# Twenty matmuls of a blank tile before the first key transposes

## The chip, the cores and the metric

The kernel runs on one core of one Trainium2 chip. A core has a matmul engine (PE, with its weight loads shown apart as PEld), a vector engine (DVE), an activation engine (ACT), a general engine (POOL), a sync engine (SP) and 16 DMA engines. The metric is the device time of one execution, in microseconds; lower is better. The time given for a kernel is the median of its runs.

## The reference

The program is an attention with two kinds of heads, followed by a two-layer network with SiLU. Batch is 8, heads 8, sequence 576, head dimension 64.

```python
scores = scale * np.matmul(q, k.transpose(0, 1, 3, 2))
rel = pos[:, None] - pos[None, :]
mask_plain = (rel >= 0) & (rel < window)                 # window = 32: heads 0-3
mask_dil = (rel >= 0) & (rel < window * dilation) & (rel % dilation == 0)   # dilation = 4: heads 4-7
scores = np.where(masks[None, :, :, :], scores, -1000000000.0)
attn = softmax(scores)                                   # max, exp, sum, divide
attn_out = np.matmul(attn, v)
...
h = x @ w_in                                             # x: 4608 x 512, w_in: 512 x 2048
g = h * (1.0 / (1.0 + np.exp(-h)))
return (g @ w_out).astype(np.float32)                    # w_out: 2048 x 512
```

`x` is the attention's output with the heads of a token side by side.

## The kernel before, in words

Only a band of the scores is not masked, so the kernel works on blocks of 32 queries by 64 keys. The code calls the plain heads z = 0 and the dilated heads z = 1; for the latter, positions are sorted into four classes by remainder, so that their masked scores become a band as well. For each batch b the kernel loads q, k and v, turns q and k so that the head dimension lies on partitions, computes block scores, takes maximum, exponential and sum, turns the probabilities, multiplies them with v, and runs the two layers on the 576 tokens.

The order of the instructions is written out by hand (`manual_schedule`): each engine executes in the order in which the code names its instructions, and waits for the tiles that it needs. From batch 1 on, the attention of the next batch is laid between the matmuls of the current batch's layers by a table of steps (`plan_of`). Batch 0 has nothing to hide behind, and its attention is written out in a straight sequence ahead of the first layer.

What happens up to the first layer, with the lines of the code before the change:

- POOL issues all loads. The first four are k and q of batch 0's dilated heads, then k and q of its plain heads (`load_one`, L112), then v (L154, L163), the four pieces of w_in (L171), q and k of batch 1 (L119, L112), the four pieces of w_out (L177) and v of batch 1. All are cast from float32 to float16 on the way.
- DVE clears a small tile `band` (L184) and the margins of the key and query tiles (L208 to L211); POOL makes the identity and the band mask.
- PE waits for the first k and transposes it (`transpose`, L258), then the first q; ACT and DVE copy the results out of PSUM (L309). `scores0` writes the mask into PSUM by a matmul with the identity (L396) and adds the scores to it (L354 for dilated heads, L338 for plain ones). DVE takes the negated maximum (L413), ACT the exponential (L519, or L508 when DVE has subtracted the maximum in `shift0`, L428), DVE the sum (L527), reciprocal and product (L538 to L541) and the turn of the probabilities (L557). PE multiplies with v (L588), and ACT or DVE copy that into `xT` (L657, L662). Batch 0 is cut into two parts of 256 and 320 tokens, and each part has both kinds of heads.
- The first layer of batch 0 (`layer1_part`, L696) goes over 256 tokens in four groups of 16 matmuls with 256 columns, one group for each piece of w_in, then over the other 320 tokens. Between its groups stand the rest of batch 0's attention and the attention of batch 1. ACT computes SiLU (L704). The second layer is `layer2_first` (L716), and L725 and L726 store the results. For later batches the layers are at L671 and L740, and scores at L327 and L338.
- `warm` (L631) issues n matmuls of the identity with itself into a PSUM tile whose content is overwritten later. The code calls it three times: 3 before the values of the first dilated part, 2 before those of the first plain part, and 3 before the first layer.

PSUM has eight banks. The pool `ps` holds four buffers of one bank, and the pool `big` two buffers of two banks, which the scores of batch 0 and the results of the layers use in turn:

```python
big = ctx.enter_context(tc.tile_pool(name="big", bufs=2, space=bass.MemoryType.PSUM))
...
band = cpool.tile([P, KB], F32, name="band")
nc.vector.memset(band[0:W], 0.0)
tiles_qk(0)
load_one(0, 1, 1)
load_one(0, 1, 0)
make_identity(nc, ident)
```

In these lines P is 128, KB is 64, W is 32, and SA, used by the change, is 256.

Of the kernel before, what the change touches and what calls it, by code (L numbers as in the profile page):

```python
# [8 lines left out]
F16 = mybir.dt.float16  # L9
F32 = mybir.dt.float32  # L10
# [6 lines left out]
P = 128  # L17
# [12 lines left out]
def kernel(  # L30
# [9 lines left out]
    nc = tc.nc  # L40
# [13 lines left out]
    SA = NS // 2  # L54
# [6 lines left out]
    cpool = ctx.enter_context(tc.tile_pool(name="const", bufs=1))  # L61
# [7 lines left out]
    big = ctx.enter_context(tc.tile_pool(name="big", bufs=2, space=bass.MemoryType.PSUM))  # L69
# [110 lines left out]
        )  # L180


    band = cpool.tile([P, KB], F32, name="band")
    nc.vector.memset(band[0:W], 0.0)  # L184
    tiles_qk(0)
# [736 lines left out]
```

## Time and profile before

| what | value |
|---|---|
| median of the runs shown | 306.98 us (306.69 to 309.01, 3 runs) |
| the profiled execution's own time | 306.95 us |
| its span, first to last instruction | 305.1 us |
| PE busy | 292.7 us, 96% of the span |
| DVE, ACT, POOL busy | 199.7, 206.4, 119.6 us |
| PE's first matmul | 5.61 us, after the first k |
| first matmul of layer 1 | 19.69 us |

The page divides the span into 40 equal slices of 7.6 us; a digit is the busy share of an engine in one slice, in tenths. The row PEclk gives the clock that was granted to PE in the same way. The page's chain is followed back from the last instruction, at each step to what released it. A line such as "L696 PE MATMUL h<-xT,w_in 128*128 128x256 f16 x14" means 14 matmuls of code line 696 that write the tile h from xT and w_in, with a weight of 128x128 and 256 moving columns. A bracket behind a line of the timeline is the idle time of the engine before it and what ended it. Matmuls overlap, so a group's length is the distance of its first and last start, and the length of one more.

### The profile page before, as it was taken

Reading aid. Unit: us, or ns where it says so; the run is one execution under the profiler, and the core shown is the slowest. Engines: PE = TensorE matmul, PEld = TensorE weight load, DVE = VectorE, ACT = ScalarE, POOL = GpSimd, SP = SyncE. Lnnn points to the kernel's source line nnn. Section 1 sums busy time; section 2 is a strip of 40 time slices with the busy share of each in tenths; the row PEclk is TensorE's granted clock in tenths of the full one; section 3 lists DMA queues with packets and bytes.
Section 4 is the critical chain, followed back from the end, with each engine's and each line's share of the span. In section 5 each row is a group of like instructions: output and inputs, shape, how many; then the busy total and the mean of one; then the engine's idle time right before and its main releaser. Section 6 shows DMA issues by size and latency. Waiting matters only on the chain.

```text
span 305.1 us, 10290 instructions
## 1 busy us (share of the span) xinstructions
PE 292.7 (96%) x4400; PEld 186.9 (61%) x4400; DVE 199.7 (65%) x354; ACT 206.4 (68%) x688; POOL 119.6 (39%) x182
## 2 busy tenths in 40 slices
PE   2889999999999999999999999999999999999995
PEld 2458654577545774477645775477644775477544
DVE  2886589538898868966895768966895762820012
ACT  2497687865999559965894559975795559546200
POOL 8745347979964295336806086250000000000000
PEclk9999999999999999999999999999999999999999
DMA  6999999999994899499949199390002001110021
GB/s 109 158 205 206 208 157 170 189 185 126 118 184 87 89 70 128 119 106 41 126 71 184 37 62 134 106 118 4 3 34 105 37 2 36 54 52 0 19 86 69
DMA packets 111805, 30.47 MB, mean 100 GB/s; under 512 B 95520, under 2 KB 107280, under 8 KB 111760
## 3 DMA queue, kind: packets, MB, share of 16 engines
q0 software_dynamic: 106432, 20.38, 80.7%
q1 hardware_dynamic: 5328, 9.44, 8.5%
q8 instruction: 34, 0.56, 0.7%
q14 instruction: 11, 0.09, 0.1%
HBM read 40.75 MB, written 9.44 MB: 164 GB/s over the span
## 4 chain that ended last, share of the span: by engine, by line
PE 69%; DMA 16%; POOL 5%; DVE 4%; ACT 3%; issue 2%; POOLq 0%
PE h L671 32%; PE o L740 31%; DMA w_out<-in_moe_w_out_dram 5%; DMA n<-in_q_dram 5%; DMA w_in<-in_moe_w_in_dram 4%; PE x L588 3%; ACT pe L519 2%; DMA n<-in_k_dram 2%; PE s L327 2%; POOL n L132 2%; POOL n L112 1%; DMA vw<-in_v_dram 1%; DVE pn L541 1%; POOL w_in L171 1%; DVE ob L725 1%
## 5 line engine op out<-in xcount | busy, mean ns | idle before, releaser
L679 ACT ACTIVATE gT<-h 128x576 f16<-128x576 f32 x112 | 73.0, 651 | 60.5 <-PE h L671 60.4
L740 PE MATMUL o<-w_out,gT 128*128 128x512 f16 (+1 forms) x528 | 113.8, 373 | 0.0
L671 PE MATMUL h<-xT,w_in 128*128 128x288 f16 x896 | 113.4, 286 | 0.0
L671 PEld LDWEIGHTS <-w_in 128*128 128x128 f16 x896 | 86.6, 98 | 23.5 <-issue 0.2
L740 PEld LDWEIGHTS <-gT 128*128 128x128 f16 x528 | 50.7, 98 | 55.4
L519 ACT ACTIVATE pe<-ms,nm 128x64 f32<-128x64 f32 x238 | 78.9, 333 | 0.1
L725 DVE COPY ob<-o 128x512 f32<-128x512 f32 (+1 forms) x35 | 22.8, 664 | 45.4 <-PE o L740 44.1
L519 ACT ACTIVATION_READ_ACCUMULATOR pe<-ms,nm 128x1 f32 x238 | 44.5, 187 | 0.0
L132 POOL DMA_DIRECT2D n<-in_k_dram x44 | 31.9, 736 | 26.2 <-DVE kC L300 25.1
L372 DVE SCALAR_TENSOR_TENSOR ms<-s,mask 128x512 f32<-128x512 f32 x28 | 19.2, 686 | 28.6 <-PE s L327 19.9
L132 POOL DMA_DIRECT2D n<-in_q_dram x44 | 31.9, 735 | 3.5 <-DMA n<-in_q_dram 3.1
L154 POOL DMA_DIRECT2D vw<-in_v_dram x32 | 18.4, 580 | 34.4 <-PE x L588 31.8
L541 DVE TENSOR_TENSOR pn<-pe,r 128x640 f16<-128x640 f32 (+2 forms) x32 | 25.3, 792 | 1.1
L557 DVE STREAM_TRANSPOSE pt<-pn 128x640 f16<-128x640 f16 (+4 forms) x32 | 24.7, 772 | 1.1
L163 POOL DMA_DIRECT2D vw<-in_v_dram x32 | 21.1, 665 | 9.7 <-DMA w_out<-in_moe_w_out_dram 8.0
L439 DVE TENSOR_REDUCE nm<-ms 128x10 f32<-128x640 f32 (+1 forms) x28 | 22.0, 786 | 1.0
L696 PE MATMUL h<-xT,w_in 128*128 128x256 f16 (+1 forms) x128 | 18.6, 302 | 0.0
L588 PEld LDWEIGHTS <-vw 32*64 32x64 f16 (+1 forms) x1264 | 13.1, 107 | 7.4 <-issue 6.7
L588 PE MATMUL x<-pt,vw 32*64 32x64 f16 (+2 forms) x1264 | 15.0, 193 | 0.9 <-DVE pt L557 0.8
L696 PEld LDWEIGHTS <-w_in 128*128 128x128 f16 x128 | 12.7, 103 | 3.9 <-issue 0.2
L623 DVE CAST xT<-x 128x288 f16<-128x288 f32 x22 | 15.0, 819 | 0.0
L716 PE MATMUL o<-w_out,gT 128*128 128x512 f16 x64 | 14.7, 380 | 0.2 <-ACT ob L725 0.2
(84 smaller groups left out, 209.7 us busy)
## 6 DMA issues: line engine op xcount, KB each, us to landing
out_dram<-ob SPq DMA_DIRECT2D x35, 256.0 KB, 3.0
n<-in_k_dram POOLq DMA_DIRECT2D x24, 108.0 KB, 4.8
n<-in_q_dram POOLq DMA_DIRECT2D x24, 108.0 KB, 5.3
vw<-in_v_dram POOLq DMA_DIRECT2D x31, 80.0 KB, 3.7
vw<-in_v_dram POOLq DMA_DIRECT2D x32, 72.0 KB, 4.0
w_in<-in_moe_w_in_dram POOLq DMA_DIRECT2D x4, 512.0 KB, 9.3
w_out<-in_moe_w_out_dram POOLq DMA_DIRECT2D x4, 512.0 KB, 11.7
n<-in_k_dram POOLq DMA_DIRECT2D x20, 72.0 KB, 3.7
```

The costliest lines, as they stand in the source:

```text
L132: nc.gpsimd.dma_start(out=qk[b, z, which][o : o + QB], in_=bass.AP((q, k)[which].tensor, (b * H + z * HH + half * HH // 2) * S * D + x * Q ...
L163: nc.gpsimd.dma_start(out=vw[h * QB : h * QB + QB, 0:NB], in_=v[b, h].rearrange("(m p) d -> p m d", p=QB))
L439: nc.vector.tensor_reduce(out=nm[:, 0:w], in_=ms[:, 0:w], axis=AX.X, op=ALU.max, negate=True)
L519: nc.scalar.activation(pe[:, t, :], src[t], AF.Exp, bias=a["nm", z, hi][:, t : t + 1], scale=k, accum_out=l[:, t : t + 1],)
L541: nc.vector.tensor_tensor(pn[:, 0:w], a["pe", z, hi][:, 0:w], r[:, 0:w, None].broadcast_to([P, w, KB]), ALU.mult)
L557: nc.vector.transpose(out, src)
L588: nc.tensor.matmul(x[h // 2][h % 2 * D : h % 2 * D + D, col : col + wd], vws[b % 2][r, NB + kb * DIL + c if z else kb], turned_cols(b, pt[ ...
L671: nc.tensor.matmul(h[:, half, 0:HS], w_in16[:, c, f * P : f * P + P], xT[:, c, half * HS : half * HS + HS], start=(c == cs[0]), stop=(c == ...
L679: nc.scalar.activation(gT[:, f, s0 : s0 + S].rearrange("p (a c) -> p a c", a=2), h[:, :, 0:HS], AF.Silu)
L696: nc.tensor.matmul(hs[i // m][:, i % m, 0 : c1 - c0], w_in16[:, c, (f + i) * P : (f + i + 1) * P], xT[:, c, c0:c1], start=(c == 0), stop=( ...
L725: copy(ob, o)
L740: nc.tensor.matmul(o[:, 0, 0:m], gT[:, f, t * P : (t + 1) * P], w_out16[:, f, cols], start=(f == 0), stop=(f == NFF - 1),)
```

## The change

Before anything else of the written-out part, the kernel allocates a float16 tile `blank` of 128 x 256, has DVE fill it with zeros, takes a buffer of the pool `big`, and has PE multiply the blank tile twenty times: a 128x128 piece of it as the weight, all 256 columns as the moving operand, into the first bank of the buffer. Nothing reads this result. The lines below it, and every other function, stay as they were and move down by five lines.

```diff
+    blank = cpool.tile([P, SA], F16, name="blank")
+    nc.vector.memset(blank, 0.0)
+    first_big = big.tile([P, 2, 512], F32, tag="big", name="blank_out")
+    for _ in range(20):
+        nc.tensor.matmul(first_big[:, 0, 0:SA], blank[:, 0:P], blank, start=True, stop=True)
     band = cpool.tile([P, KB], F32, name="band")
     nc.vector.memset(band[0:W], 0.0)
     tiles_qk(0)
```

In the order of instructions, DVE gets one more at its head, PE gets twenty weight loads and twenty matmuls at its head, and POOL, ACT and SP have the same instructions in the same order.

## The prediction

> **What bounds the kernel now.** I read the page first: the span, the slices and the chain.
>
> ```profile
> span 305.1 us, 10290 instructions
> ...
> PE   2889999999999999999999999999999999999995
> ...
> PEclk9999999999999999999999999999999999999999
> ...
> PE 69%; DMA 16%; POOL 5%; DVE 4%; ACT 3%; issue 2%; POOLq 0%
> ```
>
> PE, the matmul engine, is full from the fourth slice on; only the first three slices (0 to 23 us) and the end have holes, so whatever the change brings must be brought before 23 us. Next come PE's own waits:
>
> ```profile
> PE t L258 <- DMA n<-in_k_dram: 5.6, 1, 5.6
> PE x L588 <- DVE pt L557: 0.8, 2, 0.5
> PE t L274 <- DMA n<-in_q_dram: 0.7, 1, 0.7
> PE s L396 <- ACT pe L519: 0.4, 1, 0.4
> PE s L327 <- DVE qC L300: 0.4, 1, 0.4
> ```
>
> The first is the 5.6 us in which the change puts its work. It cannot be shortened, because it ends with k's landing; every other wait is under 1 us. Then the timeline of the first 30 us, where columns are start, length, engine, line, operation, count and the wait before:
>
> ```profile
> 0.90 0.17 DVE L208 MEMSET kC<- 128x128 uint32 x1
> ...
> 5.61 1.14 PE L258 MATMUL t<-ident,n 96*128 96x96 f16 x12 [5.61 <-DMA n<-in_k_dram]
> ...
> 12.24 0.68 DVE L527 TENSOR_REDUCE l<-pe 128x8 f32<-128x512 f32 x1
> 12.38 0.50 PEld L338 LDWEIGHTS <-qT 64*32 64x32 f16 x32 [0.79 <-DVE qT L278]
> 12.38 0.68 PE L338 MATMUL s<-kT,qT 64*32 64x64 f16 x32 [0.31 <-DVE qT L278]
> ...
> 13.12 0.69 DVE L413 TENSOR_REDUCE nm<-s 128x8 f32<-128x512 f32 x1 [0.20 <-PE s L338]
> ...
> 18.00 0.61 PE L631 MATMUL x<-ident 128*128 128x256 f16 x2
> 18.53 0.61 PE L588 MATMUL x<-pt,vw 32*64 32x64 f16 x32
> 19.07 0.82 PE L631 MATMUL h<-ident 128*128 128x256 f16 x3
> 19.69 3.23 PE L696 MATMUL h<-xT,w_in 128*128 128x256 f16 x14
> ...
> 25.43 1.92 PE L696 MATMUL h<-xT,w_in 128*128 128x256 f16 x16
> ...
> 27.29 0.53 PE L588 MATMUL x<-pt,vw 32*64 32x32 f16 x44
> ```
>
> The two L696 lines are the same matmul at two speeds. Single rows follow each other every 213 ns up to 22.73 us and every 109 ns behind it, and one lasts 417 ns before and 272 ns after. So PE runs at half speed from its first instruction to 22.77 us. The PEclk row reads 9 throughout and hides this: the trace's clock record holds nothing earlier than 22.77 us, reads full from there to 306.07 us, and half behind that. A faster clock before 22.77 is all that blank matmuls can bring.
>
> **The change part by part.**
> *The memset.* It fills 512 bytes per partition, as the quoted L208 memset does in 0.17 us. The DVE memsets behind it end near 1.76 instead of 1.59 us; their readers start at 4.71 (POOL, band) and 6.31 us (the kC copy). Cost nothing; the cover would have to shrink by 3 us.
>
> *Twenty matmuls.* The nearest rows are L631: a 128x128 weight, 256 columns, every 213 ns at the slow clock, with loads of 102 to 151 ns beside them. PE waits for the memset, which takes DVE's first place (0.81 us), so they start near 1.1 us and stream for 20 x 0.213 = 4.27 us, to 5.4 us. PE is released by k at 5.61, so 0.2 us is left. An overrun would be taken up by the waits for q: 0.24 us before the second transposes, 0.74 us before 10.84. I take zero; the bounds are 0 and 0.3 us.
>
> *The buffer.* blank_out takes the first of the two "big" PSUM buffers, so each later user takes the other one. The order of reuse is the same, and as PE alone touched the blank, no other engine must release it. Nothing. No DMA is issued, moved or waited for anew; POOL and SP keep their order.
>
> *The clock.* Two questions: does it rise, and does it stay? Neither is in the trace, so bounds. For the rise: PE ran without a hole from 12.38 to 15.1 us (2.7 us) and stayed slow, and without a hole from 16.64 to the rise at 22.7 (6.1 us). The blanks give 4.3 us, between the two. But much of both stretches uses 32 or 64 rows; of full-size work the successful one had the 3.7 us from 19.07, and 4.3 is more. I take it that it rises. For the stay: behind the last matmul, which ends at 301.8 us, the half-clock record comes at 306.07, so 4.3 us of idleness was enough to drop it. From 5.6 to 19 us the longest hole would be near 1.3 us (0.74 now, and faster work before it). I take it that it stays.
>
> The Trainium skill ("TensorE: Matmul & The Clock Gate", section "What's actually happening") says that the clock is released after one busy window of about 3.4 us, and that these windows run freely, not from the kernel's start. The trace agrees: 306.07 - 22.77 = 283.30 us is 83 windows of 3.413 us. By that rule a burst of 4.27 us holds a whole window for only a quarter of the phases, so for the others the sum would be zero unless a partly filled window is enough. The same page ("Part 4: PE-mode transpose") holds that transposes don't count as activity, and the two windows behind the blanks are mostly transposes; by it the clock could drop again, which is the second rival.
>
> *The sum with a fast clock from 5.6 us on.* Landings don't move: from its first load until 88 us POOL waits for nothing but DMAs.
> (a) Up to layer 1 the work passes through DVE and ACT. DVE gives up only its waits on PE: 0.13 us before the qT copy (11.44 to 11.57, shorter transposes) and 0.20 us before the reduce at 13.12. There L338's 32 matmuls, 0.68 us now, would take 0.41 us, as 32 of that line at 41.20 us do, but DVE's L527 then ends last. Together 0.33 us. From 13.12 to 19.19 us ACT's exponentials and DVE set the pace.
> (b) Layer 1's first 32 matmuls: the second is released at 20.00 us, and the 32nd starts at 24.61, 30 spacings in 4.61 us. At 109 ns they take 3.27, a gain of 1.34; with (a) 1.67 us.
> (c) What is late next: the last piece of w_in.
>
> ```profile
> 13.96 12.27 DMA w_in<-in_moe_w_in_dram
> ```
>
> In the chain this transfer ends at 26.23 us; the group that needs it starts at 27.74 now and would be ready at 26.07. Just before, the values at 27.29 need the DVE transpose that ends at 26.03, or 25.70 with (a); PE would be there at 25.62. These leave a start near 26.28, so **1.46 us** is gained. The second piece (20.98 us) and the third (23.35) are in time.
> (d) Behind it nothing takes it back. The next landings are early by the trace's records: batch 1's q at 29.04 against its use near 29.5, w_out's last piece at 42.41 against 51, v at 45.98 against 50.2. The chain's "DMA" up to 70.5 us is no bound: the tile of L300 had landed by 55.7, and DVE was busy with L439 until 70.6, itself behind PE's scores at 67.06. That moves along with PE.
>
> The profiled execution took 306.95 us around its span of 305.1, and the runs shown have a median of 306.98 (306.69 to 309.01), the same. 306.95 - 1.46 = **305.5 us**, 0.5% less. A measurement of this kernel tells a change from none at about 1%, so even full success lies within it.
>
> **The rivals.**
> *The clock never rises* (the change doesn't do what it says). For: 2.7 us was too little, and 4.3 is not 6.1. Against: full-size matmuls. Nothing else moves: 306.95 us.
> *It rises, drops before 19 us, and rises again as now.* For: in 5.7 to 19 us the work, once fast, fills perhaps a third of PE's time. Against: no hole is near 4.3 us. At most (a) is kept: 306.6 us.
> *It drops, and the next rise comes later than 22.77 us: slower.* The place is L696. If the second group of 16 is slow too, 17 matmuls pay 104 ns more, 1.77 us, less the 0.33 of (a): 308.4 us. It turns slower once the fast spacing begins more than about 3 matmuls (0.33 / 0.104) later than now. The one run of 309.01 says that the start of this program can vary by as much; the low 306.69 and 306.95 say that it rarely does.
>
> **How the numbers follow.** Rise 0.7 times stay 0.75: the forecast 0.53. Never rises 0.22. Rises and drops 0.12. Late rise 0.08. Left over 0.05, half of it for an overrun that costs. The forecast's own range is 304.9 (no wait in c, and a little from later stages) to 306.0 us (two thirds of it). To hold 8 in 10 the range must take in the two cases without gain and their run-to-run spread: 304.8 to 307.4 us. Over 1% faster would be under 303.9, more than full speed can give: 0.03. Over 1% slower is above 310.0, worse than the late rise: 0.04. Within 1%: 0.93.
>
> **What would show it.** In the changed kernel's profile 20 matmuls end before 5.6 us; the first L258 rows last near 206 ns instead of 281 if the clock has risen; L696 has 109 ns spacing from its first row, and no row of 417; PE waits for w_in at about 26 us; DVE's reduce at 13.12 comes at 12.8. If L696 starts slow, the clock did not rise or stay, and L258's rows tell which. I am wrong if the gain appears and is lost before 60 us, or if a landing moves.

## The result: slower, and the profile after

The changed kernel takes 309.56 us (308.32 to 313.23, 15 runs) beside 306.94 us for the kernel before on the same chip (306.15 to 310.13, 15 runs). The ratio, taken without the one run of 313.23 us, which stands apart from the others, is 1.0078, with a 95% interval of 1.0053 to 1.0103. The prediction was 305.5 us, within 304.8 to 307.4: the time is outside its range and the sign is wrong. The profiled execution took 308.45 us with a span of 306.4 us, 1.3 us more span than before.

The page of the changed kernel (the code behind the change has moved down by five lines, so L696 is L701 and so on):

```profile
span 306.4 us, 10331 instructions
...
PE   8699989999999999999999999999999999999995
...
PEclk9669999999999999999999999999999999999999
...
q8 instruction: 34, 0.56, 0.8%
```

PE now works from the first slice on. PEclk reads 6 in slices two and three, because part of each ran at half speed; the page before showed nines there only because its record held nothing so early. The q8 line, which I had not read, will turn out to be the one that matters: 34 packets and 0.56 MB of instructions.

PE's waits (total, times, longest, in us):

```profile
PE t L279 <- DMA n<-in_q_dram: 1.3, 1, 1.3
PE ss L343 <- issue: 1.2, 1, 1.2
...
PE h L701 <- issue: 0.6, 2, 0.4
...
PE s L359 <- issue: 0.3, 1, 0.3
```

The 5.6 us for k have gone, as predicted, and what the prediction did not foresee are the waits called "issue": time in which PE stood and the profile shows nothing that it waited for. The answer for this execution of the kernel before lists none. They are 2.1 us together.

The timeline of PE's first 25 us shows both the clock and the first two of these waits:

```profile
1.06 4.45 PE L187 MATMUL blank_out<-blank 128*128 128x256 f16 x20 [1.06 <-DVE band L189]
5.43 1.14 PE L263 MATMUL t<-ident,n 96*128 96x96 f16 x12
6.80 0.72 PE L263 MATMUL t<-ident,n 96*128 96x96 f16 x12 [0.23 <-DMA n<-in_q_dram]
...
10.89 0.69 PE L279 MATMUL t<-ident,n 64*64 64x64 f16 x36 [1.33 <-DMA n<-in_q_dram]
...
14.61 0.30 PE L359 MATMUL s<-kC,qC 64*32 64x64 f16 x11 [0.29 <-issue]
...
19.73 0.89 PE L701 MATMUL h<-xT,w_in 128*128 128x256 f16 x3
20.81 3.33 PE L701 MATMUL h<-xT,w_in 128*128 128x256 f16 x29 [0.18 <-issue]
```

The blanks run where they should, 1.06 to 5.4 us. The first twelve transposes take 1.14 us as before, the second twelve 0.72 us, so the clock rose between them. At 10.89 PE waits longer for q than before (1.33 against 0.74 us) and has lost its lead. And a group of L701 that should be one run of 32 matmuls breaks after its third.

The two dearest waits come later, where PE has no other hole. Before, this stretch read:

```profile
37.18 2.35 PE L696 MATMUL h<-xT,w_in 128*128 128x320 f16 x16
...
43.62 0.24 PE L338 MATMUL ss<-kT,qT 64*32 64x64 f16 x8
```

and after:

```profile
36.47 1.67 PE L701 MATMUL h<-xT,w_in 128*128 128x320 f16 x11
38.57 0.84 PE L701 MATMUL h<-xT,w_in 128*128 128x320 f16 x5 [0.44 <-issue]
...
43.36 0.23 PE L343 MATMUL ss<-kT,qT 64*32 64x64 f16 x7
44.77 0.19 PE L343 MATMUL ss<-kT,qT 64*32 64x64 f16 x1 [1.17 <-issue]
```

Sixteen matmuls on one tile pair have become 11 + 5, and eight have become 7 + 1. The profile shows no wait for data at these splits. Laying the two executions matmul against matmul, the changed kernel is 0.18 us ahead at the first transposes, 0.57 us behind at 14.61, 0.05 behind at 15.7, 0.7 to 0.75 ahead from 22 us on, 0.11 ahead at 38.57, 1.11 behind at 44.77, and 1.30 behind at the end.

**A theory from the trace: the supply of PE's instructions.** Counted from PE's first matmul as number 0, the four breaks lie at matmuls 223, 351, 735 and 863: all are 128 apart or a multiple of it. A matmul and its weight load are two instructions, so 128 of them are 256 instructions, and 8,840 matmuls and loads in pieces of 256 make 34.5 pieces, against the 34 packets of 16,384 bytes of the q8 line. So PE's program arrives in pieces, by the same DMA engines that carry the data. The trace records each packet:

| packet starts | ends | first matmul of that piece | distance | PE stood |
|---|---|---|---|---|
| after: 12.33 | 13.30 | 14.61 | 1.31 | yes |
| 18.58 | 19.54 | 20.81 | 1.27 | yes |
| 24.40 | 25.29 | 26.73 | 1.44 | no |
| 30.40 | 31.29 | 33.02 | 1.73 | no |
| 36.37 | 37.32 | 38.57 | 1.25 | yes |
| 42.40 | 43.35 | 44.77 | 1.42 | yes |
| before: 24.74 | 25.69 | 27.60 | 1.92 | no |
| 30.97 | 31.91 | 33.91 | 2.01 | no |
| 37.34 | 38.31 | 39.64 | 1.33 | no |
| 43.28 | 44.24 | 47.90 | 3.66 | no |

PE goes on some 1.3 us after the packet's end where it had to stand, and a distance well above that means that it arrived later than its instructions. The breaks of every run below that has any lie at 223 plus a multiple of 128, so the ends for the kernel before are taken there too. In this stretch a packet starts after PE has crossed into the piece before it: 3.35 us after in the case of 36.37 (PE crossed at 33.02), 3.83 in that of 42.40 (38.57). Between 212 and 249 us, where the page's DMA row reads 0 to 2, it starts between 0.1 us before the crossing and 1.0 us behind it in the kernel before, and between 1.8 us before and 1.0 behind in the changed kernel. This fits a sequencer that reads ahead of the matmuls; how far it does the trace doesn't show. The packet at 24.74 in the kernel before came only 1.0 us behind its crossing (23.73). So around 40 us a piece takes 5.5 to 6.2 us from crossing to crossing (33.02 to 38.57 to 44.77), and one that holds small matmuls, which PE does in less, makes it stand. Forty instructions at the head move all crossings by 20 matmuls: a piece that covered 8.26 us of work before (39.64 to 47.90, with long L716 matmuls) now ends ahead of most of these and covers 5.0 (38.57 to 43.6, where PE stands). The Trainium skill ("Runtime: NRT & Kernel Launch", section "Instruction fetch mechanics") describes such blocks of 16 KiB and 256 instructions, and calls the cost of crossing their boundary mostly hidden. The spacing of 128 agrees; "hidden" holds here for most pieces, and not for the ones named.

The rivals: that the blanks' clock does the harm (a rise and a drop cost more than the steady half speed), and that the loss lies elsewhere, near 88 us, where the spread of the runs suggested a second cause.

### The profile page after: what moved, and what is told of

The parts are those of the page before. It is cut to its first block, busy times and chain, and to the rows that moved or that the text cites. A ratio compares the mean times of both kernels' runs of the same rounds, so it can differ in the third digit from the quotient of the medians.

```text
span 306.4 us, 10331 instructions
## 1 busy us (share of the span) xinstructions
PE 295.6 (96%) x4420; PEld 188.4 (61%) x4420; DVE 200.1 (65%) x355; ACT 206.1 (67%) x688; POOL 119.7 (39%) x182
## 4 chain that ended last, share of the span: by engine, by line
PE 68%; DMA 17%; POOL 5%; DVE 4%; ACT 3%; issue 2%; POOLq 0%
PE h L676 32%; PE o L745 31%; DMA n<-in_q_dram 5%; DMA w_out<-in_moe_w_out_dram 5%; DMA w_in<-in_moe_w_in_dram 4%; PE x L593 3%; DMA n<-in_k_dram 2%; ACT pe L524 2%; PE s L332 2%; POOL n L132 2%; POOL n L112 1%; DMA vw<-in_v_dram 1%; DVE pn L546 1%; POOL w_in L171 1%; DVE ob L730 1%
## 5 line engine op out<-in xcount | busy, mean ns | idle before, releaser
L524 ACT ACTIVATION_READ_ACCUMULATOR pe<-ms,nm 128x1 f32 x238 | 44.4, 187 | 0.0
L154 POOL DMA_DIRECT2D vw<-in_v_dram x32 | 18.4, 581 | 34.1 <-PE x L593 32.4
L562 DVE STREAM_TRANSPOSE pt<-pn 128x640 f16<-128x640 f16 (+4 forms) x32 | 24.7, 772 | 1.1
L701 PE MATMUL h<-xT,w_in 128*128 128x256 f16 (+1 forms) x128 | 17.8, 290 | 0.6 <-issue 0.6
L701 PEld LDWEIGHTS <-w_in 128*128 128x128 f16 x128 | 12.1, 99 | 4.3 <-issue 1.2
```

The costliest lines, as they stand in the source:

```text
L524: nc.scalar.activation(pe[:, t, :], src[t], AF.Exp, bias=a["nm", z, hi][:, t : t + 1], scale=k, accum_out=l[:, t : t + 1],)
L562: nc.vector.transpose(out, src)
L701: nc.tensor.matmul(hs[i // m][:, i % m, 0 : c1 - c0], w_in16[:, c, (f + i) * P : (f + i + 1) * P], xT[:, c, c0:c1], start=(c == 0), stop=( ...
```

## The experiments

Each ratio is to the kernel before on the same chip, with its 95% interval; it is not the quotient of the medians, and differs from it by up to 0.2%. The medians of the kernel before in the four sets were 307.97, 306.97, 308.24 and 307.89 us.

**1. Instructions without warmth.** Twenty and forty multiplications of 32 rows, 64 columns and 32 moving columns, too small to fill anything (pad20, shown here; pad40 has `range(40)`):

```diff
+    for _ in range(20):
+        nc.tensor.matmul(first_big[0:HF, 0, 0:W], blank[0:W, 0:HF], blank[0:W, 0:W], start=True, stop=True)
```

> Twenty multiplications of the blank tile stay at the head of PE, but each is as small as it can be (32 rows, 64 columns of weight, 32 moving columns), so PE is busy for about 1 us there and the clock has no reason to rise early. PE has the same 40 instructions more than before. Theory S (instruction supply: PE's instructions come in pieces of 16 KB, 128 matmuls with their loads, one about every 6 us while the DMA queues are full, and 40 more at the head make PE run out of them near 39 and 44 us): as slow as the changed kernel, 308.5 to 309.5 us, with waits of PE called issue near 38.6 and 44.8 us, together 1.5 to 2.6 us. Theory C (the clock: it rises, drops, and its next rise comes later than before): 306.9 us, as before, without such waits.

Measured: 309.39 us, ratio 1.0051 (1.0025 to 1.0076). The clock's record begins at 20.76 us, so it never rose early, and PE's waits of pad20 are those of the changed kernel:

```profile
PE ss L343 <- issue: 1.2, 1, 1.2
PE h L701 <- issue: 1.1, 2, 0.7
```

The breaks are at the same matmuls, and the time is as expected from supply. Warm or not, 40 more instructions at the head are enough for the loss.

> As pad20, with forty such small multiplications, so 80 instructions more than before. Theory S, laying the places of the pieces' ends on the matmuls' times of before: the piece that PE needs at 37.0 us is there at 39.6 us, so 2.6 us are lost: 309.0 to 310 us. Theory C: 306.9 us.

Measured: 310.28 us, 1.0072 (1.0042 to 1.0103). The time is 0.3 us above the expected range, and the place is another one: a wait of 0.4 us at 14.34, one of 1.7 us at the multiplications with v (20.54 us), and none near 39 us. With the crossings moved 20 matmuls further, another piece is the short one.

**2. Blanks without more instructions.** The changed kernel, with 20 of the 32 score matmuls of batch 0's first dilated part left out (some 0.3 us of work near 8.5 us), so that from there on each piece ends where it does in the kernel before:

```diff
-                            score_class(0, h, 2 * e + m, 2 * part + t, sd[:, m, e * n + t], False)
+                            if part or (2 * t + e) * 8 + 2 * h + m >= 20:
+                                score_class(0, h, 2 * e + m, 2 * part + t, sd[:, m, e * n + t], False)
```

> All twenty blank matmuls of the changed kernel stay, and 20 of the 32 score matmuls of the first dilated part are left out (so these scores are only the mask for most blocks): PE has exactly as many instructions as before ahead of everything that follows. The left-out matmuls would take about 0.3 us near 8.5 us, ahead of a wait for q. Theory S: no waits called issue near 38 and 44 us, 306.0 to 307.2 us. Theory C: the clock drops and rises as in the changed kernel, 308.5 to 309.5 us.

Measured: 307.19 us, 0.9995 (0.9964 to 1.0026); the only "issue" wait among PE's first is 0.2 us. The blanks are all there, and the loss is gone. The gain is not shown either: the interval leaves room for 0.36%, not for the 0.48% that was forecast. The profiled execution is the shortest of all (305.72 us, span 304.0); its PE was 1.51 us ahead of the kernel before at matmul 420 (25.31 us there) and still 1.13 ahead at the end.

**3. Half as many blanks, of 512 columns.**

```diff
+    blank = cpool.tile([P, 2 * SA], F16, name="blank")
+    for _ in range(10):
+        nc.tensor.matmul(first_big[:, 0], blank[:, 0:P], blank, start=True, stop=True)
```

> Ten blank matmuls of 512 columns instead of twenty of 256: the same 4.3 us of full-size work on PE, half of the extra instructions (20). Theory S, from the places of the pieces' ends on the matmuls' times of before: at most 0.1 us is lost, 306.2 to 307.3 us. Theory C: the clock does as in the changed kernel, 308.5 to 309.5 us.

Measured: 307.18 us, 0.9987 (0.9954 to 1.002), as expected from supply: the clock again rose for one window, with 20 instructions less, and there is no "issue" wait at all. The profiled execution took 310.54 us, though, and shows what else can go wrong in this kernel. Its timeline around 88 us:

```profile
87.33 2.44 DVE L546 TENSOR_TENSOR pn<-pe,r 128x640 f16<-128x640 f32 x1
...
88.02 1.05 POOL L499 TENSOR_TENSOR ms<-ms,nm 128x512 f32<-128x512 f32 x1
...
90.70 0.61 PE L593 MATMUL x<-pt,vw 32*64 32x64 f16 x48 [1.83 <-DVE pt L562]
```

and the same place in the kernel before:

```profile
86.95 0.83 DVE L541 TENSOR_TENSOR pn<-pe,r 128x640 f16<-128x640 f32 x1
...
88.82 1.05 POOL L494 TENSOR_TENSOR ms<-ms,nm 128x512 f32<-128x512 f32 x1
```

The DVE product lasts 2.44 instead of 0.83 us where POOL's subtraction falls beside it. PE then stands for 1.83 us, and its clock drops for one window, 91.29 to 94.70 us. In pad20 the subtraction (87.97 to 89.03) meets DVE's L543, which takes 1.21 instead of 0.15 us; in pad40 0.69 us. It is POOL's only arithmetic there, and it stands in POOL's queue behind the loads of batch 4's q and k, so its moment depends on when those can be issued. The Trainium skill ("SBUF — State Buffer", section "Who interferes with whom") says that a DVE instruction with two inputs in SBUF contends with a POOL instruction that reads SBUF. The trace agrees for the product, which reads two tiles, with the 2.44 us. The sentence does not cover L543, which reads one tile, and why the product lost 1.61 us beside a subtraction of 1.05 us is not shown.

**4. Is the scatter this collision?** In both kernels POOL's subtraction was given to DVE:

```diff
-            at(21, shift, 3, 0, 0, nc.gpsimd)
+            at(21, shift, 3, 0, 0)
```

> The kernel before with one thing else: the only arithmetic that POOL does behind the start, the subtraction of the maximum for batch 3's plain heads (L494, 1.05 us on POOL near 88 us), is done by DVE. Theory P (where POOL's subtraction falls on a DVE operation that reads and writes SBUF, DVE stands still until it ends; POOL is placed by the landings of its DMAs and DVE by PE, so this is a throw of dice): the subtraction costs DVE 0.7 us ahead of the values of batch 2, so about 307.3 to 307.8 us, but the runs lie close together, without the upper half of the spread of before (308 to 310 us). Without theory P: the spread of before stays, 0.7 us higher.

> The changed kernel with the same edit. Theory S (instruction supply): slower than b_dve by the 1.2 to 1.8 us of the issue waits, 308.7 to 309.5 us, and more closely together than the changed kernel's runs. If only the collision of POOL and DVE made the changed kernel slow: the same as b_dve.

Measured: without blanks (b_dve) 307.76 us (306.53 to 308.17), 1.0006 (0.9983 to 1.003); with blanks (a_dve) 308.97 us (308.15 to 310.91), 1.0057 (1.0033 to 1.0081). Both medians are within what was expected. Without blanks the spread of 4 us shrinks to 1.6; with blanks it is still 2.8. The difference of the two medians, 1.2 us, is close to the wait at L343, which is 1.0 us here.

**5. The number, or the place of the ends?** 128 tiny multiplications at the head are 256 instructions, one whole piece, and move no end of a later piece:

```diff
+    for _ in range(128):
+        nc.tensor.matmul(first_big[0:W, 0, 0:W], blank[0:W, 0:W], blank[0:W, 0:W], start=True, stop=True)
```

> The head of PE gets 128 multiplications as small as 32 x 32 x 32, 256 instructions more than before, exactly one piece of 16 KB, so the ends of the pieces lie on the same matmuls as before. Theory S: no loss, 306.9 us within the spread of before, or up to 0.3 us more if these matmuls take longer than k's load; the number of added instructions does not matter, only where the pieces end. If the loss grew with the number of added instructions: 6.4 times that of the changed kernel, over 315 us.

Measured: 307.36 us, 1.0005 (0.9982 to 1.0028); one "issue" wait of 0.5 us, at 27.33, where PE had come 0.97 us earlier than in the kernel before. More than six times as many added instructions cost nothing that the runs can tell (at most 0.28%), so the place of the ends decides and not their number.

**6. What a clock that stays up would bring.** Ten 512-column blanks and 18 more between the stages of batch 0's attention, with 28 score matmuls left out to pay for the instructions, and POOL's subtraction on DVE as in experiment 4. `keep(n)` is n blanks; between the stages stand 2, 2, 5 and 2, and `values0` warms with 8 and 4 instead of 3 and 2. Two lines of the edit:

```diff
+    keep(10)
...
+    keep(2)
```

> DVE subtracts as in b_dve, and PE gets ten blank matmuls of 512 columns at its head, eleven more of them in the holes up to 12 us, and seven more of the identity matmuls ahead of the values; 28 of the 32 score matmuls of the first dilated part are left out, so that the count of PE's instructions is that of before. Theory K (the clock drops because the work between 7 and 19 us is too thin; filled up, it stays): no half-clock record behind the first rise, layer 1 starts at 109 ns spacing, and 1.0 to 1.5 us less than b_dve. Theory S adds that the piece that PE needs at 39.6 us comes no earlier, so that much of this gain waits there: 0 to 1 us less than b_dve.

Measured: 308.12 us, 1.004 (1.0011 to 1.0068). The clock stayed up from 4.13 to 17.79 us, dropped for one window, and was full again from 21.20, but PE stood 1.1 us for a piece that it reached at 27.15 us and got at 28.24. The median is 0.36 us above that of b_dve, where 0 to 1 us less was expected: a miss. The faster start made PE reach the same piece earlier (it had been 0.64 us ahead of the kernel before at 25 us), and the piece came later than there (its packet ended at 26.88 us, not at 25.69).

**7. Fewer instructions.** If only the number of instructions counted, leaving matmuls out should only help. `lean` is the kernel before with the subtraction on DVE and 48 score matmuls of the second dilated part left out; `hold_lean` does the same to `hold`:

```diff
-                            score_class(0, h, 2 * e + m, 2 * part + t, sd[:, m, e * n + t], False)
+                            if not part:
+                                score_class(0, h, 2 * e + m, 2 * part + t, sd[:, m, e * n + t], False)
```

> b_dve with all 48 score matmuls of the second dilated part left out (those scores are only the mask), so PE has 96 instructions less ahead of everything behind 14 us and the ends of the pieces come 48 matmuls later. The clock is as before. Theory S: at the matmuls' times of before each piece is then there at least 1.7 us early instead of 0.04, but PE has nothing to gain from it while its clock rises at 20 to 25 us: 307.2 to 307.8 us, as b_dve.

> hold with the same 48 score matmuls left out, so it has as many instructions as lean, and differs from it by the blank matmuls and by the 28 score matmuls of the first part. Theory S with K (the blanks raise and hold the clock, but in hold the gain waited for instructions): now the gain shows, 1.0 to 1.5 us less than lean, and no wait called issue between 20 and 45 us. If the held clock is worth nothing by itself, as hold's time seems to say: the same as lean or slower.

Measured: lean 308.87 us, 1.0026 (1.0001 to 1.0051), hold_lean 309.36 us, 1.0035 (1.0005 to 1.0065). Both are misses. lean has "issue" waits of 1.0 us at L354 (36.33) and 0.4 us at L589, hold_lean one of 1.1 us at L362 (37.02). My expectation had taken the packets as if they came on a cadence of their own, so that PE with fewer instructions would be ahead less often. They come on PE's crossings: leaving 48 matmuls out moves the ends as adding does, and puts a stretch of small matmuls into one piece. A program with less work became slower, though its interval (1.0001 to 1.0051) only just says so. That a held clock is worth something by itself was not shown by either kernel.

**8. The collision removed by order.** POOL's subtraction comes behind the loads of batch 4 in step 17 of the plan; these were moved to step 22, once alone and once with 100 tiny multiplications at the head:

```diff
-            at(17, load_qk, 4)
+            at(22, load_qk, 4)
```

> The kernel before with one step moved: the loads of batch 4's q and k are issued five steps later, behind POOL's subtraction instead of ahead of it. Theory P: POOL then subtracts near 82.6 us, as soon as its operands are there, and always beside the same DVE operations (L372, L439), so the collision is no throw of dice any more; the loads have over 20 us of room. The runs lie close together at 306.2 to 306.8 us, or, if the fixed neighbour is a bad one, close together up to 1 us higher.

> late_qk4 with 100 multiplications of 32 x 32 x 32 at the head of PE, which end before k lands. Theory S: PE passes the end of its first piece at about 4 us instead of 10.9 us, so one more piece is fetched early, and the ends of all later pieces come as if 28 matmuls were taken away; every piece is there over 0.7 us early. Executions whose clock rises early then keep what they gain: the same as late_qk4 or up to 0.5 us less.

Measured: 307.07 us (306.87 to 307.95), 0.9966 (0.9939 to 0.9992), and with the 100 multiplications 308.27 us, 1.0017 (0.9993 to 1.0041). The runs of late_qk4 lie close together, with a median 0.3 us above what was expected. The 100 were meant to have every piece there early; instead there were waits at 36.53, 42.45 and 64.06 us of 0.59, 0.29 and 0.54 us, a miss for the same reason as lean. late_qk4 itself, which adds no instruction to PE, has an "issue" wait of 0.61 us at 28.04: the kernel before has little room too, and another execution of it can stand where the one profiled did not.

**9. Does the data on the DMA engines delay the packets?** So far this was only read off the packets' starting times. The changed kernel without the four loads of w_out (512 KB each by the page), with zeros written there by DVE at the head:

```diff
+    nc.vector.memset(w_out16, 0.0)
...
-    for c in range(4):
-        load_w_out(c)
```

> The changed kernel without the four loads of w_out (2 of the 4 MB of float32 weights): DVE fills the tile with zeros at the head instead, so the second layer multiplies with zeros and the stored result is zero. PE has the same instructions in the same places as in the changed kernel. Supply of PE's instructions, slowed by full DMA queues: with some 10 us of DMA work less before 45 us, the instruction packets that begin at 36.37 and 42.40 us in the changed kernel begin within 1.5 us of PE's crossing of the piece before, the wait of 1.2 us at the single score matmul of L343 (44.8 us) falls under 0.4 us, and the time is about 1 us below the changed kernel's, 307 to 308. Rival (a piece of PE's instructions takes 5.6 us and more whatever the DMA queues hold): the wait stays at 1.0 to 1.3 us.

Measured: 309.51 us, 1.0049 (1.0014 to 1.0083). The mechanism came as supply has it, the time did not. The timeline of PE around 40 us:

```profile
37.74 2.35 PE L700 MATMUL h<-xT,w_in 128*128 128x320 f16 x16
...
44.19 0.24 PE L342 MATMUL ss<-kT,qT 64*32 64x64 f16 x8
```

The sixteen and the eight are whole again, with PE's instructions in the same places as in the changed kernel. The packets start 1.07 us (35.36) and 2.28 us (41.53) behind PE's crossings (34.29 and 39.25), where they were 3.35 and 3.83; the second is more than the 1.5 expected. The two pieces take 4.96 and 4.98 us from crossing to crossing instead of 5.55 and 6.20. From 22 to 44.4 us this kernel makes up 1.81 us on the changed kernel. But it lost more than a microsecond at its head: q landed at 8.37 instead of 6.75 us (DVE wrote its zeros from 1.87 to 5.34 us; whether that is the reason was not tested), and PE was 1.27 us behind the changed kernel at 22.1 us. And 0.49 us went again at 90 us, where POOL's and DVE's operations met (POOL's subtraction at 84.91, the DVE product begun at 85.16 lasting 1.36 us). The rival that a piece always takes 5.6 us falls by the packets, the shorter pieces and the missing waits; the time did not show it.

**10. Blanks with the collision out of the way.** The move of experiment 8 alone (late2), with the change (a_late), and with the change and 20 score matmuls left out (same_late):

> The kernel before with batch 4's loads at step 22 once more, as the yardstick of this set, because its time should be the narrowest: 307.0 to 307.2, and 0.3 to 0.4% below the kernel before. If that gain was luck, it is 0.9985 to 1.0015 of it.

> The changed kernel with one step of the plan moved: the loads of batch 4's q and k are issued at step 22 instead of 17, so that POOL's subtraction is no longer held up behind them beside DVE's work at 88 us. The supply of PE's instructions up to 45 us is that of the changed kernel: the wait at L343 stays, 1.0 to 1.3 us, and the time is 1.2 us above the kernel before with the same move (307.07 in the set before): 308.3. If the changed kernel's loss came from the collision at 88 us, it is 307.1.

> The blanks, with 20 of the 32 score matmuls of the first dilated part left out, so that PE's instructions end their pieces where they do in the kernel before, and batch 4's loads at step 22. Supply: no wait for instructions over 0.3 us up to 60 us, and the time of the kernel before with the same move, 307.0 to 307.2; if the faster first part is kept, down to 306.3. If blanks cost time for another reason than their number of instructions: 308.3.

Measured: late2 307.46 us (306.88 to 308.75), a_late 308.90 us (308.38 to 309.87), same_late 307.35 us (306.31 to 308.14); to the kernel before 1.0003 (0.9981 to 1.0025), 1.0021 (0.9988 to 1.0055) and 0.9986 (0.9958 to 1.0014). To late2, whose runs scatter less, a_late stands at 1.0041 (95% interval by resampling ten runs each: 1.0026 to 1.0055), same_late at 0.9987 (0.9969 to 1.0004). So the change costs 1.4 us with the collision moved out of the way, and its blanks cost nothing that these runs can tell where the ends stay in place. The wait at L343 in a_late is 0.6 us, less than the 1.0 to 1.3 expected; the stand at L701 before it is 1.3 us. The breaks in a_late, at 128 matmuls each or a multiple again:

```profile
14.63 0.30 PE L359 MATMUL s<-kC,qC 64*32 64x64 f16 x11 [1.02 <-issue]
...
21.10 3.33 PE L701 MATMUL h<-xT,w_in 128*128 128x256 f16 x29 [1.23 <-ACT pe L524]
...
39.69 0.84 PE L701 MATMUL h<-xT,w_in 128*128 128x320 f16 x5 [1.26 <-issue]
...
45.33 0.19 PE L343 MATMUL ss<-kT,qT 64*32 64x64 f16 x1 [0.63 <-issue]
```

The second is put down to ACT, but it is matmul 351, the one at 20.81 in the changed kernel, and comes 1.33 us behind its packet's end (18.81 + 0.96). late2 did not repeat the gain of late_qk4, and its traced execution has "issue" waits of 0.24 us (34.53) and 0.39 us (40.72) with no instruction added. The two ratios together leave at most a few tenths of a per cent, so no version here is shown to beat the kernel before.

## Why the prediction was wrong, step by step

*The memset and the twenty matmuls.* Right: they run from 1.06 to 5.4 us, and k, which landed at 5.38, found PE free at 5.43.

*"No DMA is issued, moved or waited for anew; POOL and SP keep their order."* This is the step that failed. The data landings up to layer 1 moved by 0.3 us at most, but PE's own instructions are DMA traffic too, and 40 more of them moved the ends of all its pieces by 20 matmuls. The term, set at nothing, measured 1.4 us (a_late against late2), and 1.2 us in a_dve against b_dve. It shows as breaks at matmuls 223, 351, 735 and 863. The first two cost little, because DVE or the earlier clock made it good; those at 38.57 and 44.77 us lie where PE has no slack.

*Does the clock rise?* Right. The first row at the faster rate is in the second twelve transposes, and the clock's record begins with full speed at 6.91 us. In 14 of the 15 runs of the changed kernel the mean clock is 0.967 to 0.983, which a record with a rise and a drop gives; in the one with 1.000 (309.47 us) it did not rise early. The prediction's other estimate, that only a quarter of the phases would do if a whole window of blanks were needed, did not come true: in the profiled execution the window that ended at 6.91 had begun at 3.50, with blanks up to 5.4 us and transposes behind them, and that was enough.

*Does it stay?* Wrong. The table by windows of the changed kernel (length, then busy time of PE, PEld, DVE, ACT and POOL, each with its count, and the granted clock):

```profile
6.91:10.33 3.42, 1.96 (x82) 1.27 (x81) 2.60 (x7) 1.65 (x4) 2.59 (x5) 1.00 1.18 172
10.33:13.74 3.41, 2.54 (x72) 1.32 (x72) 2.41 (x4) 1.13 (x2) 2.61 (x4) 0.50 1.90 155
13.74:17.15 3.41, 2.68 (x86) 1.55 (x85) 3.17 (x10) 2.99 (x18) 3.29 (x6) 0.50 1.10 162
17.15:20.57 3.42, 3.42 (x82) 2.10 (x81) 3.30 (x7) 3.42 (x23) 0.72 (x1) 0.50 1.24 207
```

The clock was up for exactly one window and was half for three. I had argued from holes: none was near the 4.3 us that dropped it at the end. No hole in that window or across its end was longer than 1.33 us, so holes are not the reason here. What fits is how little the window holds: 1.96 of 3.42 us, transposes and small products. That is my second rival's reason (its "perhaps a third" was 57%), and its outcome for the clock. The fillers of hold kept the clock up for three windows more, which agrees; what share of which matmuls is enough was not measured.

*(a), 0.33 us up to layer 1.* Not seen. PE was 0.61 us ahead at 7.45 us, and gave it back at 10.89, where it waited 1.33 us for q, which landed at 10.85, as before (10.80).

*(b), 1.34 us in layer 1.* About half of it came in the profiled execution, by another way: the clock rose for good at 20.57 instead of 22.77 us, since its window fell so, and PE was 0.75 us ahead at 24 us.

*(c) and (d), "nothing takes it back".* Wrong by the same omission. From 38.57 to 44.77 us the lead of 0.71 us turned into a lag of 1.11 us. The kernel before has little room itself: it came to matmul 735 (39.64) only 1.33 us behind its packet's end, while the stands of the changed kernel ended 1.25 to 1.42 us behind theirs. But a lead is not lost there by necessity, since a packet follows an earlier crossing: same_count, with its ends where the kernel before has them, passed matmul 735 at 38.57, 1.07 us earlier and without a wait, its packet having come 0.97 us earlier (36.37). With unmoved ends the leads were cut at an earlier piece, at matmul 479 (27.60 us in the kernel before): by 0.17 us of waiting in same_count, 1.09 in hold.

*The rivals.* "It rises, drops, and rises again as now" had the clock right and a time that was 1.5 us too low for the profiled execution (306.6 against 308.45). The slower rival, a late rise at L696, did not happen in the profiled execution, where the rise came earlier (20.57 against 22.77 us). The sentence "I am wrong if the gain appears and is lost before 60 us" was met, at 38.57 and 44.77.

*The size.* The medians differ by 2.6 us, the profiled executions by 1.5 in time and 1.3 in span; 1.4 is what supply explains with the collision gone. The rest is in the scatter of the two kernels, of which the collision at 88 us is one cause seen in the traces. The mean clocks on record say a little more. Of the 133 runs of the kernel before in the four sets, 12 have 0.994, which is one window of half speed more (as in ten512 behind 91.29 us); all 12 took 309.85 us or more, and none of the other 121, whose median is 307.6, took longer than 309.85. No run of b_dve, late_qk4 or late2 has it. The changed kernel's 15 runs go by the clock too: 308.45 and 309.13 us at 0.983, the three half-speed windows of the profiled execution; 308.32 to 310.08 at about 0.977, four; 310.4 to 310.81 at 0.972, five; 313.23 at 0.967, six. So the profiled execution is one of the mildest. Whether the added windows are a later rise or a drop at the collision the mean clock doesn't tell: a_dve and a_late have runs at 0.972 as well, and with blanks the clock rose for good as late as 22.97 (a_dve) and 23.23 us (same_late). A late rise in some runs thus stays open as part of the loss.

## What to carry to other kernels

Adding instructions to an engine that is full need not be free even where their run time is hidden: they move the points at which its next block of instructions must have arrived. Where a timeline breaks a group of like matmuls with "issue", count the distance of the breaks; a multiple of 128 matmuls is the sign. What removed the waits here was putting the ends back where they had been (same_count, pad128 but for 0.5 us) or fewer data DMAs beside them (a_zero_out), not just fewer instructions; none of it is shown to beat the kernel before. Look at more than one execution: a piece that is just in time in one is late in the next. A burst that warms the clock is worth only what the work behind it keeps warm and what no landing takes back.

## What the runs showed of the hardware

- PE's instructions come in packets of 16,384 bytes over the same DMA engines as data. Between 24 and 45 us, with the DMA row at 9, a packet started 3.35 to 3.85 us behind PE's crossing in the traces of the kernel before and the changed kernel (but for the one named), in the quiet stretch at most about 1.0 us behind it, and where PE had stood it went on 1.25 to 1.5 us behind the packet's end (1.6 in one short stand of late2). What fills these 1.3 us stays open.
- Every kernel with full-size blanks at its head raised the clock early in its profiled execution, and none without them did. In all of these but two the early rise lasted one window of 3.41 us; with fillers three (hold_lean, 5.72 to 15.96 us) and four (hold, 4.13 to 17.79). The Trainium skill ("TensorE: Matmul & The Clock Gate", section "What's actually happening") has such free-running windows, and the records agree, with lengths of 3.41 us or multiples. By its "Part 4: PE-mode transpose" transposes don't count as busy in the same way. In the kernel before, a window with 3.16 us of transposes and small scores (5.7 to 9.1 us) was not followed by a rise, while one of late_qk4 with 3.09 us, with five 128-row products of the identity among it (16.93 to 20.34 us), was; that fits, but no run here separates transposes from small scores.
- Without blanks, or behind the drop, the clock rose between 18.4 and 24.7 us in all kernels that have a record of it, whatever was at their head. Two executions of one and the same kernel, late_qk4 and late2, had it at 20.34 and 22.07 us.
- Beside one POOL subtraction of 1.05 us a DVE product of 0.83 us, begun 0.69 us before it, lasted 2.44 us.
